# Attention scored and normalised for two groups of queries at a time, over 88 columns for each 32 queries instead of 118 for each 64, with the value products two visits behind the scores

## The chip, the cores and the metric

The kernel runs on one core of a Trainium2 chip. The metric is the device time of one execution in microseconds (us). It is given as the median of three runs. The profile comes from one further execution, recorded by the hardware profiler; its span runs from the first to the last instruction. Engines are called as the profile calls them: PE (matrix products), PEld (its weight loads), DVE, ACT, POOL, and SP, which only issues transfers (DMAs).

## The reference

Inputs are q, k, v of 4 batches, 8 heads, 768 positions and 64 dimensions, and two weight matrices, 512x2048 and 2048x512. All are float32.

```
k_sum = max of k over blocks of 32 positions         # 24 per head
v_sum = mean of v over the same blocks               # 24 per head
scores_l = scale * q @ k.T      where |i - j| < 16, else -1e9
scores_s = scale * q @ k_sum.T + log(32)
a = softmax([scores_l, scores_s])
attn = a @ [v, v_sum]                                # 3072 tokens x 512
out = relu(attn @ w_in)**2 @ w_out
```

So a query sees 31 keys around it and 24 block maxima.

## The kernel before

**Groups, units, visits.** A group is 64 queries of one batch, all 8 heads; there are 48 groups, 12 in each batch. Eight groups make a unit of 512 tokens, and there are six units. The feed-forward layer goes over one unit at a time. Units 0 and 1 run plainly: for each of 16 slices f of the hidden width, FI (12 matmuls, `h`), then on ACT and DVE `r`, `gh` and `gl` (the high and the low part of the squared relu), then FO (12 matmuls into `o`). Units 2 to 5 run as two pairs through a scheme of seven products (FI `h` in L1203, FP `o` in L1317). The attention of later groups runs between them. One *visit* on PE computes the scores S of one pair of groups (L597) and the value products V of the pair before (L803). Between S and V of one pair stands the softmax:

- M (DVE, L676): scale, add the mask, copy from the score tile `att` into `p`
- X (DVE, L692): the maximum of a row
- E (ACT, L728): the exponential, one instruction for each row block, with its sum read out
- R (DVE, L740, L741): the inverse of the sum; N (DVE, L747): its product with `p`
- T (DVE, L776): transposes of 32x32 squares from `p` into `a`
- TW and TR (SP, L787, L793): store the squares of `a` to DRAM as `turn`, and fetch them back in the order in which V needs them

A group has 4 row blocks of 128 rows (two heads of 64 queries), each with 118 columns: 24 block maxima and the 94 keys that 64 queries can see. A pair therefore has 8 row blocks in two tiles `p`, two M pieces for each group, and two each of X, N and T. The columns of the second group of a pair come from a copy `kw` of its keys (KW, ACT, L621 and L622), and the maxima are moved along in `kb` by POOL (KC, L610), so that 118 columns stand side by side for each group. Groups 0 to 7 go first, alone, with the mask added by PE; groups 8 and 9 are scored alone too, into the `o` tiles.

**What sets the order.** All work is entered as tasks in a planner (`Plan`), with a cost, a key (due time from `wanted(g)`), tasks it comes after, and buffers that it takes or uses. The planner then writes one fixed order for every engine. Each engine works its list strictly in this order, waiting at semaphores; SP is one such list for all transfers. The keys and values of a batch (`batch_k`, `batch_v`) are loaded once per batch: KL loads `kb` after the last scores of the batch before, KM (DVE, L430) makes the maxima; VM on PE (L498) makes the 24 means of v.

The weights come as 64-bit words. DVE and ACT turn each slice into a high and a low part during unit 0 (L916 to L933: WM, WR, WJ, WH, WW), beside the first 14 groups' softmax.

## Time and profile before

| | |
|---|---|
| runs | 600.46, 600.50, 600.58 us; median 600.5 us |
| profiled execution, span | 599.2 us (the runs hold some 1.3 us more around the span) |
| PE busy | 584.1 us, 97% of the span |
| DVE busy | 379.7 us, 63% |
| ACT busy | 354.8 us, 59% |
| mean granted PE clock | 0.997 of full speed |

The profiled execution has no time beside its span. A busy share is the time in which at least one instruction of the engine is under way. The granted clock is what the chip let PE have in a stretch, 1.00 for 2.4 GHz and 0.5 for 1.2 GHz. In the views, "idle before <-X" says what ended the idle time.

### The profile page before, as it was taken

Reading aid. Unit: us, or ns where it says so; the run is one execution under the profiler, and the core shown is the slowest. Engines: PE = TensorE matmul, PEld = TensorE weight load, DVE = VectorE, ACT = ScalarE, POOL = GpSimd, SP = SyncE. Lnnn points to the kernel's source line nnn. Section 1 sums busy time; section 2 is a strip of 40 time slices with the busy share of each in tenths; the row PEclk is TensorE's granted clock in tenths of the full one; section 3 lists DMA queues with packets and bytes.
Section 4 is the critical chain, followed back from the end, with each engine's and each line's share of the span. In section 5 each row is a group of like instructions: output and inputs, shape, how many; then the busy total and the mean of one; then the engine's idle time right before and its main releaser. Section 6 shows DMA issues by size and latency. Waiting matters only on the chain.

```text
span 599.2 us, 11513 instructions
## 1 busy us (share of the span) xinstructions
PE 584.1 (97%) x4132; PEld 477.3 (80%) x4132; DVE 379.7 (63%) x670; ACT 354.8 (59%) x866; POOL 66.1 (11%) x117
## 2 busy tenths in 40 slices
PE   8989999989999999999999999999999999999997
PEld 6778888858888888888878787788888888888885
DVE  5999997757547814225755958977541552349753
ACT  2999886657646635467735556656564743455542
POOL 4300004233455200000000000000000000000000
PEclk9999999989999999999999999999999999999999
DMA  8999956859987884735857956889833762126672
GB/s 307 332 392 316 371 205 211 274 162 364 343 292 249 277 282 151 264 106 151 282 157 211 291 177 205 269 257 291 276 98 105 217 209 102 35 84 203 194 231 98
DMA packets 94428, 135.43 MB, mean 226 GB/s; under 512 B 9676, under 2 KB 50636, under 8 KB 94372
## 3 DMA queue, kind: packets, MB, share of 16 engines
q1 hardware_dynamic: 94372, 134.70, 68.6%
q8 instruction: 33, 0.54, 0.4%
q14 instruction: 23, 0.19, 0.1%
HBM read 98.22 MB, written 35.65 MB: 223 GB/s over the span
## 4 chain that ended last, share of the span: by engine, by line
PE 83%; DVE 7%; ACT 5%; DMA 3%; SPq 1%; issue 1%; POOL 0%; DVEq 0%; POOLq 0%; ACTq 0%
PE h L1203 28%; PE o L1317 24%; PE o L1003 11%; PE h L979 11%; PE x L803 3%; PE att L597 2%; DMA raw<-wW 2%; PE warm L397 1%; ACT p L728 1%; DVE nm L692 1%; DMA a<-turn 1%; DVE w L933 1%; PE vps L498 1%; DVE t L925 1%; ACT w L930 1%
## 5 line engine op out<-in xcount | busy, mean ns | idle before, releaser
L1203 PE MATMUL h<-xh,w 128*128 128x512 f32 x448 | 138.8, 391 | 0.5 <-ACT r L1213 0.5
L1317 PE MATMUL o<-gh,w 128*128 128x512 f32 x448 | 120.9, 391 | 0.4 <-ACT gh L1301 0.4
L1306 DVE TENSOR_TENSOR gl<-g,gh 128x512 fp32r<-128x512 f32 x112 | 75.9, 686 | 38.3 <-ACT gh L1301 38.2
L1203 PEld LDWEIGHTS h<-xh,w 128*128 128x128 f32 x448 | 83.5, 188 | 18.7 <-ACT r L1213 1.3
L1317 PEld LDWEIGHTS o<-gh,w 128*128 128x128 f32 x448 | 83.5, 188 | 18.4 <-ACT gh L1301 0.9
L1301 ACT CAST gh<-g 128x512 fp32r<-128x512 f32 x112 | 68.8, 620 | 48.2 <-DVE gl L1306 24.9
L1203 PE MATMUL h<-xl,w 128*128 128x512 f32 x224 | 87.2, 389 | 0.0
L1213 ACT ACTIVATE r<-h 128x512 f32<-128x512 f32 x64 | 38.0, 596 | 77.9 <-PE h L1203 64.6
L979 PE MATMUL h<-xh,w 128*128 128x512 f32 x240 | 74.3, 391 | 0.0
L728 ACT ACTIVATE p<-p,nm 128x118 f32<-128x118 f32 x160 | 61.1, 387 | 17.1 <-DVE nm L692 17.0
L1317 PE MATMUL o<-gl,w 128*128 128x512 f32 x224 | 69.5, 391 | 1.0 <-DVE gl L1306 0.9
L1003 PE MATMUL o<-w,gh 128*128 128x512 f32 x240 | 62.7, 398 | 2.5 <-ACT gh L990 2.5
L1003 PEld LDWEIGHTS o<-w,gh 128*128 128x128 f32 x240 | 45.1, 190 | 12.4 <-ACT gh L990 2.9
L676 DVE SCALAR_TENSOR_TENSOR p<-att,mask 128x236 f32<-128x236 f32 x76 | 26.5, 395 | 44.1 <-PE att L597 43.9
L979 PEld LDWEIGHTS h<-xh,w 128*128 128x128 f32 x240 | 44.8, 188 | 9.6 <-DVE xl L870 0.3
L1317 PEld LDWEIGHTS o<-gl,w 128*128 128x128 f32 x224 | 41.8, 188 | 10.7 <-DVE gl L1306 2.2
L1203 PEld LDWEIGHTS h<-xl,w 128*128 128x128 f32 x224 | 42.0, 188 | 8.8
L979 PE MATMUL h<-xl,w 128*128 128x512 f32 x120 | 46.7, 389 | 0.0
L993 DVE TENSOR_TENSOR gl<-r,gh 128x512 fp32r<-128x512 f32 x30 | 22.4, 749 | 34.0 <-ACT gh L990 30.2
L610 POOL COPY kb<-kb 128x96 f32<-128x96 f32 x25 | 8.5, 339 | 293.0 <-ACT kw L622 121.4
L988 ACT ACTIVATE r<-h 128x512 f32<-128x512 f32 x30 | 17.9, 596 | 32.9 <-PE h L979 32.9
L1003 PE MATMUL o<-w,gl 128*128 128x512 f32 x120 | 34.0, 393 | 0.3 <-DVE gl L993 0.3
(148 smaller groups left out, 842.0 us busy)
## 6 DMA issues: line engine op xcount, KB each, us to landing
raw<-wW SPq DMA_DIRECT2D x32, 512.0 KB, 7.3
w<-scr_s SPq DMA_DIRECT2D x64, 256.0 KB, 2.8
w<-scr_a SPq DMA_DIRECT2D x48, 256.0 KB, 3.6
turn<-a SPq DMA_DIRECT2D x160, 64.0 KB, 2.2
a<-turn SPq DMA_DIRECT2D x40, 256.0 KB, 4.1
w<-scr_i SPq DMA_DIRECT2D x40, 256.0 KB, 3.0
v<-vS SPq DMA_DIRECT2D x33, 192.0 KB, 3.8
kb<-kT SPq DMA_DIRECT2D x16, 384.0 KB
```

Source lines behind the costliest of these rows:

```text
L676: nc.vector.scalar_tensor_tensor(out=pr.tile[:, j, :KEYS], in0=x, scalar=SCALE, in1=mask_of(g)[0].unsqueeze(1).broadcast_to([P, x.shape[1] ...
L728: nc.scalar.activation(x, score_tile(g, p % parts)[:, p] if by_pe else x, AF.Exp, bias=nm.tile[:, p : p + 1], scale=SCALE if by_pe else 1. ...
L803: nc.tensor.matmul(x_of(i)[h % 2 * D : (h % 2 + 1) * D, h // 2, :], lhsT=v_bufs[g].tile[:KEYS, h * D : (h + 1) * D], rhs=av[:KEYS, 2 * c : ...
L979: nc.tensor.matmul(cut(h), lhsT=lhs.tile[:, k * P : (k + 1) * P], rhs=rhs[:, k, c0 : c0 + n], start=(i == 0), stop=(i == 3 * KT - 1),)
L988: t2 = add(f"RL{name}", "ACT", act, lambda: nc.scalar.activation(cut(r), cut(h), AF.Relu), due + 3, [t1], take=[r], use=[h])
L993: lambda: nc.vector.tensor_tensor(out=cut(gl), in0=cut(r), in1=cut(gh).bitcast(F32), op=ALU.subtract),
L1003: nc.tensor.matmul(o_of(o, t), lhsT=terms[i][0].tile[:, (t - t0) * P : (t - t0 + 1) * P], rhs=terms[i][1].tile, start=(first and i == 0), ...
L1203: nc.tensor.matmul(h.tile, lhsT=lhs.tile[:, k * P : (k + 1) * P], rhs=rhs[:, k, c0 : c0 + TU], start=(i == 0), stop=(i == 3 * KT - 1),)
L1213: t2 = add(f"RL{name}", "ACT", 0.56, lambda: nc.scalar.activation(r.tile, h.tile, AF.Relu), due + 3, [t1], take=[r], use=[h])
L1301: f"GH{s}_{n}", "ACT", 0.54, lambda x=x, gh=gh: nc.scalar.copy(out=gh.tile, in_=x.tile), due - 4, ready,
L1306: lambda x=x, gh=gh, gl=gl: nc.vector.tensor_tensor(out=gl.tile, in0=x.tile, in1=gh.tile.bitcast(F32), op=ALU.subtract),
L1317: nc.tensor.matmul(o.tile[:, d], lhsT=chunk.tile[:, w * HALF + d * P : w * HALF + (d + 1) * P], rhs=y.tile, start=begins and w == 0 and y ...
```

## The change

- From group 8 on, the two groups of a pair share one softmax. The score tile has 8 blocks of 128 rows, and each row block holds four times 32 queries. Each 32 queries see 88 columns: 24 maxima and 64 keys. A matmul scores 32 queries of one head against 128 columns, given as two runs of 64 keys in `ends` (`kb` with 40 columns in front): the first run ends in the 24 maxima and begins with 40 columns that nobody reads.
- One M, X, N and T for the pair and eight E; `p` is a single tile, transposed at 96 columns. `turn` takes 3 of 4 blocks of squares per store, 4 stores for the pair, two fetches; the blocks that stay zero are cleared once at the start (4 transfers).
- KW is gone, KC is gone for groups after 6. One half mask of 88 columns replaces the third mask; windows at the edge of a batch are masked by two DVE memsets.
- From pair (14, 15) on (`DEEP`), values come two visits behind the scores: S of (14, 15) stands alone, each later visit has S of pair n and V of pair n-2, and two V stand alone at the end. Keys move by `AHEAD`, and the sums of v (`SUMS_AT`) stand at other visits.

```diff
+AHEAD = 21.0
+DEEP = 14
+SUMS_AT = 0, 0, 2, -2
...
+            if g % 2:
+                p_bufs[g] = buf("p", 1, (P, H, 3 * SQ), F32, f"p{g}", fixed=True)
+                a_bufs[g] = buf("a", 2, (P, 2 * DM), F32, f"a{g}", fixed=True)
...
+    def pair_keys(rows, p, k0):
+
+        x = ends[rows, p * (NB + S) : p * (NB + S) + HALF_W]
+        return bass.AP(x.tensor, x.offset, [x.ap[0], [FRONT + NB + k0, 2], [1, HALF_W]])
+
+    def pair_scores(both):
+
+        for i, g in enumerate(both):
+            k0 = TQ * (g % NW) - WINDOW + 1
+            for h in [(p, p + 1) for p in range(0, NPAIR, 2)]:
+                for half in range(2):
+                    for p in h:
+                        for r in range(2):
+                            a, m, c = square_of(2 * p + r, i)
+                            rows = slice(r * D, (r + 1) * D)
+                            first = c * TQ + half * SQ
+                            nc.tensor.matmul(
+                                s_bufs[g][0].tile[first : first + SQ, a, m * P : (m + 1) * P],
+                                lhsT=q_bufs[g].tile[rows, p, half * SQ : (half + 1) * SQ],
+                                rhs=pair_keys(rows, p, k0 + half * SQ), start=True, stop=True,
+                            )
...
+        def masked():
+            nc.vector.scalar_tensor_tensor(
+                out=pr.tile[:, :, PAD:], in0=pair_tile(g)[:, :, FRONT:], scalar=SCALE,
+                in1=half_mask.unsqueeze(1).broadcast_to([P, H, COLS]), op0=ALU.mult, op1=ALU.add,
+            )
...
+        t_e = [add(f"E{g}_{n}", "ACT", 0.36, lambda n=n: exps(n), due - 12 + 0.1 * n, [t_x], use=[pr, nm]) for n in range(H)]
...
+        def store():
+            for i in range(NSQ):
+                to = d.tile[::2, :, i, :] if i % 2 else d.tile[:3, :, i, :]
...
-            deps += keys_of(then[0], range(NPAIR)) + [t_QL[then[1]], window(then[1])] + [t_T[g] for g in both]
+            deps += keys_of(then[0], range(NPAIR)) + [t_QL[then[1]]]
...
+                if g == DEEP:
+                    scores_first([g, g + 1])
+                else:
+                    i = g - (2 if g < DEEP else 4)
+                    visit([i, i + 1], [g, g + 1], sums)
+                pair_softmax([g, g + 1])
                 done_g += 2
                 if done_g == NG:
+                    visit([g - 2, g - 1])
                     visit([g, g + 1])
```

Three places show what the planner makes of it. The first is PE late in unit 0, where pair (14, 15) is scored. `att` is the score tile, `x` what V writes, `gh_12` the high part of slice 12. Before:

```order
L1003 MATMUL o_67<-w_1253,gl_11_1491 128x512 x2
L1003 MATMUL o_66<-w_1253,gl_11_1491 128x512 x2
L597 MATMUL att_68<-kb,q_1057 64x118
L597 MATMUL att_69<-kb,q_1057 64x118
...
L803 MATMUL x_1540<-a_1409,v_83 64x64 x8
L803 MATMUL x_1540<-a_1433,v_84 64x64 x8
```

Now:

```order
L1131 MATMUL o_66<-w_1194,gl_9_1346 128x512 x2
L1131 MATMUL o_67<-w_1194,gl_9_1346 128x512 x2
L676 MATMUL att<-kb,q_1364 32x128 x16
L676 MATMUL att<-kb,q_1373 32x128 x16
L1107 MATMUL h_10_1444<-xh,w_1037 128x512 x2
```

These scores moved from behind FO of slice 11 to behind FO of slice 9 and stand without a V. 32 matmuls of 32 queries and 128 columns replace 16 of 64 and 118.

The second place is ACT, where the same pair's exponentials (E) stand among the feed-forward layer's work (`r`, `gh`). Before:

```order
L930 CAST w_1536<-t_1513 128x2x512
L1088 CAST cr_1484<-cs_1485 128x1024
L867 CAST xh<-x_1540 128x4x128
L621 COPY kw_1596<-kb 128x4x24
L622 COPY kw_1596<-kb 128x4x94
L728 ACTIVATE p_85,nm_81<-p_85,nm_81 128x118 x4
L728 ACTIVATE p_86,nm_79<-p_86,nm_79 128x118 x4
L988 ACTIVATE r_13_1634<-h_13_1576 128x512
```

Now, the next pair's exponentials (16, 17) at the place where r of slice 13 is made:

```order
L1118 CAST gh_12_1576<-r_12_1542 128x512
L1116 ACTIVATE r_13_1579<-h_13_1526 128x512
L1216 CAST cr_1514<-cs_1515 128x1024
L1117 ACTIVATE r_13_1579<-r_13_1579 128x512
L1118 CAST gh_13_1635<-r_13_1579 128x512
L995 CAST xh<-x_1584 128x4x128
L856 ACTIVATE p_80,nm_83<-p_80,nm_83 128x88 x5
```

Before, r and gh of slice 13 are queued behind eight exponentials; now they stand ahead of them, and the two KW copies are gone.

The third place is SP, with the stores of one pair's squares (`turn`) and the last weights (`raw`). Before:

```order
L913 DMA raw_1406<-wW 128x512
L913 DMA raw_1406<-wW 128x512
L787 DMA turn_1427<-a_1409 32x4x128 x4
L787 DMA turn_1435<-a_1433 32x4x128 x4
L913 DMA raw_1456<-wW 128x512
```

Now:

```order
L1041 DMA raw_1438<-wW 128x512
L593 DMA q_1457<-qW 128x256
L593 DMA q_1460<-qW 128x256
L1041 DMA raw_1463<-wW 128x512
L887 DMA turn_85<-a_81 32x3x256 x4
L1041 DMA raw_1463<-wW 128x512
```

Four stores stand between the last weights where there were eight.

## Rows read from the trace of the kernel before

**Rows 1.** The page: busy time and share, PE to POOL.
```profile
PE 584.1 (97%) x4132; PEld 477.3 (80%) x4132; DVE 379.7 (63%) x670; ACT 354.8 (59%) x866; POOL 66.1 (11%) x117
```
**Rows 2.** Windows of 20 us: busy us (instructions) by engine, clock, DMA share, GB/s.
```profile
20.00:40.00 20.00, 16.83 (x301) 14.21 (x302) 19.66 (x52) 19.75 (x71) 3.29 (x9) 1.00 0.96 353
...
60.00:80.00 20.00, 20.00 (x89) 16.54 (x90) 19.92 (x32) 17.30 (x38) 0.00 (x0) 1.00 0.96 330
...
120.00:140.00 20.00, 17.25 (x123) 13.20 (x122) 13.05 (x22) 10.59 (x30) 8.44 (x10) 0.91 0.66 215
...
300.00:320.00 20.00, 19.53 (x141) 15.98 (x140) 12.49 (x25) 9.24 (x28) 0.00 (x0) 1.00 0.63 190
320.00:340.00 20.00, 19.51 (x141) 15.68 (x140) 12.42 (x22) 11.12 (x30) 0.00 (x0) 1.00 0.75 224
...
360.00:380.00 20.00, 18.63 (x177) 14.59 (x175) 18.61 (x36) 13.10 (x37) 0.78 (x2) 1.00 0.70 220
380.00:400.00 20.00, 19.90 (x142) 15.97 (x141) 17.26 (x34) 12.57 (x33) 0.27 (x1) 1.00 0.81 249
```
**Rows 3.** The same view of two windows of 2 us.
```profile
124.00:126.00 2.00, 2.00 (x7) 1.47 (x5) 1.97 (x2) 1.97 (x3) 1.56 (x2) 0.55 0.35 96
126.00:128.00 2.00, 1.71 (x6) 1.01 (x5) 2.00 (x4) 0.09 (x1) 0.00 (x0) 0.60 0.25 66
```
**Rows 4.** Chain that ended last, 105 to 127 us: start, us, what.
```profile
104.62 5.53 DMA raw<-wW
...
115.47 1.14 DVE cs L1091
116.61 0.62 DVE p L676 x2
117.23 0.60 DVE xl L870
117.83 0.56 DVE nm L692
...
118.42 3.12 ACT p L728 x16
...
126.10 0.66 DVE gl L993
```
**Rows 5.** Who waited for whom: PE's longest wait.
```profile
PE o L1003 <- ACT gh L990: 2.5, 1, 2.5
```
**Rows 6.** Chain that ended last: a visit, the sums of v, a lone V.
```profile
57.90 0.97 PE att L597 x32
58.87 1.08 PE x L803 x32
59.95 2.94 PE h L979 x12
62.90 2.72 PE o L1003 x12
...
227.24 1.44 PE vps L498 x48
```
**Rows 7.** PE matmuls of line 597 under way (x), in windows of 0.03 us.
```profile
57.80:57.83 0.03, 0.00 (x0) 1.00 0.72 273
57.83:57.86 0.03, 0.03 (x4) 1.00 1.23 478
```
**Rows 8.** Groups of instructions: busy us, mean ns of one, idle before.
```profile
L676 DVE SCALAR_TENSOR_TENSOR p<-att,mask 128x236 f32<-128x236 f32 x76 | 26.5, 395 | 44.1 <-PE att L597 43.9
L692 DVE TENSOR_REDUCE nm<-p 128x4 f32<-128x472 f32 x40 | 25.3, 635 | 0.3
L728 ACT ACTIVATE p<-p,nm 128x118 f32<-128x118 f32 x160 | 61.1, 387 | 17.1 <-DVE nm L692 17.0
L747 DVE TENSOR_TENSOR p<-p,nm 128x472 f32<-128x472 f32 x40 | 28.5, 713 | 1.0
L776 DVE STREAM_TRANSPOSE a<-p 128x512 f32<-128x512 f32 x40 | 28.3, 708 | 1.1 <-issue 0.4
L622 ACT COPY kw<-kb 128x376 f32<-128x376 f32 x19 | 9.7, 510 | 0.0
```
**Rows 9.** PE in time, 37 to 39 us: start, us, what [idle before <-releaser].
```profile
37.83 0.50 PE L979 MATMUL h_0b<-xh,w 128*128 128x256 f32 x2 [0.80 <-ACT xh L867]
```

More of the change, by code (lines that the diff above doesn't have):

```diff
@@ L34 @@
 FIRST_S = 10
-PE_MASKS = 8
 SINGLE = 3
@@ L266, in h_buf @@
         return buf("h", 2, (P, cols), F32, name, ps)
-    att = [ps.tile([P, 2, 256], F32, name=f"att{i}", bufs=1) for i in range(2)]
+    att = ps.tile([P, 2, DM], F32, name="att", bufs=1)
     def s_buf(name):
@@ L396, in mm @@
         def mm():
[L397 to L399 removed]
+            nc.tensor.matmul(x.tile, lhsT=ident(), rhs=ident(), start=True, stop=True)
+        add(f"Y{i}", "PE", 0.42 if i < COLD else 0.22, mm, 1000 + i, [t_ident], take=[x], use=[first])
     for i in range(WARM):
@@ L597, in scores @@
                         nc.tensor.matmul(
-                            score_at(g, part, j)[c * TQ : (c + 1) * TQ, :],
-                            lhsT=q_bufs[g].tile[rows, p, :] if term else unscale[rows, :],
-                            rhs=(
-                                mask_of(g)[0][rows, :] if not term
-                                else windows[g].tile[rows, p, :] if g in windows else kb[rows, p, k0 : k0 + KEYS]
-                            ),
-                            start=term, stop=not (by_pe and term),
-                        )
+                            score_tile(g, part)[c * TQ : (c + 1) * TQ, j, :],
@@ L607, in move @@
     def move(g):
[L609 removed]
+        k0, nxt = (first_key(w, S) for w in (g % NW, g % NW + 1))
         nc.gpsimd.tensor_copy(out=kb[:, :, nxt : nxt + NB], in_=kb[:, :, k0 : k0 + NB])
[L612 to L624 removed]
@@ L692, in most @@
                 nc.vector.tensor_reduce(
-                    out=m, in_=score_tile(g, i)[:, js] if by_pe else pr.tile[:, js, :KEYS], op=ALU.max, axis=AX.X, negate=True
+                    out=m, in_=score_tile(g, i)[:, js], op=ALU.max, axis=AX.X, negate=True
                 )
-                if by_pe and not one:
+                if not one:
                     nc.vector.tensor_scalar_mul(m, m, SCALE)
             t_x.append(add(
-                f"X{name}", "DVE", 0.07 + 0.48 / parts + 0.2 * (by_pe and not one), most, due - 13, [t_m[-1]],
-                take=[] if i else [nm], use=[x] + [nm] * bool(i),
+                f"X{name}", "DVE", 0.07 + 0.48 / parts + 0.2 * (not one), most, due - 13, [t_s],
+                take=[] if i else [nm], use=[s] + [nm] * bool(i),
             ))
@@ new lines, in softmax, with turn, turned @@
+        at_ps = h_buf(f"t{g}")
+        def turn():
+            for p in range(NPAIR):
+                nc.tensor.transpose(
+                    out=at_ps.tile[:, p * P : (p + 1) * P], in_=pr.tile[:, p, :], identity=ident()
+                )
+        t_T[g] = add(f"T{g}", "PE", 0.5, turn, due - 9, [t_n, t_ident], take=[at_ps], use=[pr, first])
+        def turned():
+            nc.scalar.copy(
+                out=a.tile.rearrange("k (i n r) -> k n i r", i=NSQ, n=NPAIR),
+                in_=at_ps.tile.rearrange("k (n i r) -> k n i r", n=NPAIR, i=NSQ),
+            )
@@ L843, in products @@
                     mm()
-            for g in then:
-                scores(g, range(NPAIR), False)
+            if then:
+                pair_scores(then)
             values(both, x_of)
@@ L853, in visit @@
             block_sums_done(t_v)
-        for f in means_too:
-            f()
+        waiting.extend(means_too)
+        if then and then[-1] // NW in t_VS:
+            for f in waiting:
+                f()
+            waiting.clear()
         for g in then:
```

334 lines of the change are left out of this document (200 added, 134 removed).

## Prediction

> **What bounds the kernel now.** I read the page's busy line first. PE is busy 584.1 of 599.2 us [rows 1]; DVE and ACT have a third of the span free. Only what PE does, waits for, or does at half clock can move the time.
>
> The table of windows comes next. Between 20 and 40 us PE is busy 16.83 us, so it idles 3.17, while DVE and ACT are busy 19.66 and 19.75 of 20. From 40 us on, PE idles in five windows only: 2.75 (120 to 140), 0.47 and 0.49 (300 to 340), 1.37 and 0.10 (360 to 400), together 5.18 us [rows 2]. Between 60 and 80 us DVE is busy 19.92 and PE does not wait: a full DVE alone is no loss.
>
> The stall at 120 to 140 is the largest. The waits name PE's `o` of L1003, held 2.5 us by ACT's `gh` [rows 5]. Behind it the granted clock is 0.55 and 0.60 for two windows of 2 us [rows 3], mostly the lower level, 1.2 GHz; PE had idled before it fell. The clock thus cost (1 - 0.55) x 2.00 + (1 - 0.60) x 1.71 = 1.6 us more, and the place 2.75 + 1.6 = 4.3 us in all.
>
> The chain of waits says how the stall comes about [rows 4]. A weight transfer takes 5.53 us. DVE works on it (`cs`, up to 116.6), and only then comes to M, `xl` and X of the pair just scored. The eight exponentials run on ACT from 118.42 for 3.12 us, and `r` and `gh` of slice 13 are queued behind them; `gl` ends at 126.8. The stall belongs to a softmax wedged into the feed-forward layer's chain on ACT.
>
> **The change part by part.**
>
> *Scores on PE.* Now a scoring is 32 matmul records (16 matmuls) in 0.97 us. The sums of v are 48 records of 128 columns in 1.44 us [rows 6]. Both run four tiles at once: in one window of 0.03 us four records of L597 start, none being under way in the window before [rows 7]. So 8 rounds of 118 columns take 0.97 and 12 of 128 take 1.44. With a fixed part a and b for a round of 128 columns: a + 8 x (118/128) x b = 0.97 and a + 12b = 1.44, which gives b = 0.10 and a = 0.22. The new scoring is 64 records of 128 columns in tiles half as wide. If eight run at once, it is 8 rounds again: 0.22 + 8 x 0.102 = 1.03, or 0.06 more. There are 19 scorings of pairs: +1.1. V keeps its matmuls (1.08 [rows 6]). One burst more stands in the order, because a lone S and two lone V replace one lone V. Leaving a burst costs the FI behind it 2.94 - 2.72 = 0.22 us [rows 6]: +0.2, bounds 0 and 0.44, since entering may cost as much. The term is +1.4 in all.
>
> No row shows eight tiles. The lower bound for a scoring is no addition. The upper bound is a record's mean now, 0.97/32 = 30 ns, with 64 of them: 1.94 us, +0.97 each, +18.4 in all. I take +0.06, since four starts inside 0.03 us [rows 7] show that the tiles do not queue behind one issue of 30 ns. The Trainium skill ("TensorE: Matmul & The Clock Gate", section "Wait — 56ns, not 53.3ns?") says otherwise: starts never come closer than about 25 ns, however few the columns. The window with four starts in 0.03 us [rows 7] contradicts it for separate tiles; no row here tests it for eight.
>
> *DVE.* Per pair now: 4 M of 0.395, 2 X of 0.635, 2 N of 0.713, 2 T of 0.708 [rows 8], 5.69 us. Columns per row fall from 8 x 118 = 944 to 8 x 88 = 704 (M, X, N) and from 1024 to 768 (T): by the column 4.26 us, 1.4 less, and half as many instructions can only lower it. Over 20 pairs that frees 28 us or more on DVE. On the time it counts at nothing by itself: PE's own work covers it, as it covers the full DVE at 60 to 80 us [rows 2].
>
> *ACT.* The 160 exponentials stay but shrink from 118 to 88 columns: between 0.387 (all fixed) and 0.387 x 88/118 = 0.289 us each [rows 8], so 0 to 16 us less; I take 4, near the upper price, because a small instruction's time is mostly fixed. The KW copies go: 19 x 0.510 = 9.7 us for the larger of the two [rows 8]. This too is hidden, except where ACT is waited for, which is the stall.
>
> *The stall.* In the new order `r` and `gh` of slice 13 stand ahead of the next pair's exponentials on ACT, the KW copies that stood there are gone, and four stores on SP instead of eight stand between the last weights. With values two visits behind, the V of a visit no longer needs the softmax that has just begun. The steps from `cs` to `gl` [rows 4] then leave PE's path: -4.3 us, since without the idle PE keeps its clock. The bounds are -4.3 and 0 (the wait stands elsewhere, the second rival).
>
> *The other waits of PE.* They are 5.18 - 2.75 = 2.4 us [rows 2]. Those from 300 to 400 us lie where a visit meets late inputs; one visit more (and a shorter DVE chain) should take most: -1.5, bounds -2.4 and 0.
>
> *New waits.* The lone S of (14, 15) is put behind FO of slice 9, and its exponentials fall near `gh` of slices 10 and 11. They are at worst 8 x 0.387 = 3.1 us [rows 8] in front of an FO. While they run, PE has an FI of 2.94 [rows 6] to cover all but 0.2. The keys of the next batch also have to land sooner, since S runs ahead of V by a visit while it still follows the batch's last S. I allow +1.0 for both, bounds 0 and the old stall's 4.3.
>
> *Startup.* `h_0b` waits 0.80 us for `xh` on ACT [rows 9], and 3.17 idle lies in that window. Groups 8 and 9 are now one pair: fewer DVE instructions and no KW. Against it, four transfers that clear `turn` stand on SP ahead of the first weights, and the shared M, X, N and T give their first result later than the first of two halves did. I take -0.5, bounds -2.5 (the larger part of the 3.17) and +1.
>
> *Sum.* 599.2 + 1.4 - 4.3 - 1.5 + 1.0 - 0.5 = 595.3 us of span. The profiled execution has no time of its own beside its span; the runs' median is 1.3 us above it. That makes 596.5 us for the runs. With the small terms at half their bounds, this case's own range is 594 to 599.
>
> **The rivals.**
>
> *First, the tiles: slower.* Records in eight narrow tiles start no faster than now on average, 30 ns. A scoring then takes 1.94 us, and 18.4 replaces 1.1: 595.3 + 17.3 + 1.3 = 613.9 us. It decides from the point where a scoring costs (600.5 - 596.5)/19 = 0.21 us above my 1.03, that is from 1.24. For it: 0.97/32 and 1.44/48 are both 30 ns per record [rows 6], whatever the columns. Against it: four starts in one 0.03 us window [rows 7], and the slightly longer round that 128 columns need explains both numbers as well. By the Trainium skill's 25 ns (the same page and section) a scoring would cost 64 x 25 = 1.6 us, 0.57 above 1.03, and the run an estimated 607 us.
>
> *Second, the wait comes back.* Two visits of delay and earlier keys fill SP and ACT at other moments, and one stall of the old size (2.75 idle and 1.6 of clock) stands at another place, most likely between slices 10 and 14 or where the batch's keys change. The time is 596.5 + 4.3 = 600.8 us; with none of the other waits gone 602.3, and with two places 605. For it: DVE and ACT are still full up to about 120 us, and one late `gh` costs its idle and then the clock [rows 3, 5]. Against it: 1.4 us or more of each pair leave DVE just there, and 0.5 us of KW leave ACT.
>
> *Third, more goes.* All waits after 40 us vanish (-5.18 and the clock's 1.6), no new one comes, and startup gives its 2.5: 599.2 + 1.4 - 6.8 - 2.5 + 1.3 = 592.6 us. For it: DVE and ACT bound the startup [rows 2], and both get less work. Against it: the weight transfers, which the change leaves as they are, stand at the head of the chain [rows 4].
>
> **How the numbers follow.** The forecast has 56%, the tiles 9%, the returning wait 26%, and the larger gain 9%. A measurement of this kernel can tell about 0.2%, or 1.2 us, from no change. Faster (under 599.3) are the larger gain, nearly all of the forecast and a fifth of the second rival: 0.70. Within 0.2% is about half of the second rival: 0.13. Slower are the rest of it and the tiles: 0.17. The range of 593.0 to 602.0 leaves out the tiles, the second rival's upper third and half of the third's.
>
> **What would show it.** In the profile after, a scoring in the chain should take 1.0 to 1.1 us; 1.24 or more means the first rival. PE's busy time should be 584.1 + 1.4 - 1.6 = 583.9 us. Between 120 and 140 us PE should be busy over 19.5 of 20 at a clock of 1.00, and no wait of `o` on `gh` should exceed 1 us. If one of some 2.5 us stands at another slice with a clock below 0.7 behind it, the second rival holds. M, X, N and T of a pair should sum to at most 4.3 us. Between 20 and 40 us PE's idle should be 2 to 4 us; under 1 speaks for the third rival. The forecast is wrong in its core if the stall is gone and the time is still above 599.

## The result, and the profile after

On one chip, side by side, the changed kernel takes 605.21 us (median of 20 runs) and the kernel before 601.22 us (20 runs). The ratio is 1.0061, with a 95% interval of 1.0042 to 1.0079: slower by 0.6%. The forecast was 596.5 us, with a range of 593.0 to 602.0; the measured time lies outside the range, and the sign was wrong. The profiled execution took 605.35 us with a span of 603.6 us, so it stands for the median; its span is 4.4 us above the 599.2 of before. One execution, the profiled one of best_guess, took 1172.79 us; it is left out of all numbers below.

The page of the kernel after, with busy time and share, to be read against [rows 1]:

```profile
PE 585.8 (97%) x4772; PEld 479.8 (80%) x4772; DVE 343.3 (57%) x526; ACT 340.6 (56%) x828; POOL 61.4 (10%) x101
```

DVE lost 36 us of work and ACT 14, and yet the kernel became slower. Next come windows of 20 us in the columns of [rows 2], then four of 2 us and one of 80 in the same view:

```profile
20.00:40.00 20.00, 14.25 (x310) 12.09 (x311) 14.61 (x40) 16.07 (x57) 2.46 (x4) 0.93 0.83 290
40.00:60.00 20.00, 20.00 (x99) 17.55 (x98) 18.36 (x30) 18.45 (x44) 0.00 (x0) 0.90 0.88 322
...
100.00:120.00 20.00, 17.02 (x175) 13.30 (x177) 13.93 (x21) 15.23 (x49) 2.88 (x4) 1.00 0.73 242
120.00:140.00 20.00, 18.10 (x227) 14.23 (x208) 11.79 (x15) 8.86 (x27) 8.91 (x8) 1.00 0.81 262
300.00:320.00 20.00, 20.00 (x217) 16.47 (x216) 12.72 (x21) 12.39 (x38) 0.00 (x0) 1.00 0.87 297
360.00:380.00 20.00, 20.00 (x176) 16.35 (x175) 18.04 (x29) 13.26 (x36) 0.00 (x0) 1.00 0.79 230
...
36.00:38.00 2.00, 1.02 (x19) 0.59 (x17) 2.00 (x6) 1.75 (x4) 0.00 (x0) 0.75 1.03 418
38.00:40.00 2.00, 1.56 (x18) 1.45 (x19) 0.64 (x2) 1.22 (x3) 0.00 (x0) 0.50 1.02 412
40.00:42.00 2.00, 2.00 (x11) 2.00 (x10) 2.00 (x6) 1.71 (x4) 0.00 (x0) 0.50 1.02 413
42.00:44.00 2.00, 2.00 (x11) 2.00 (x11) 2.00 (x4) 1.54 (x3) 0.00 (x0) 0.54 1.07 405
...
20.00:100.00 80.00, 74.25 (x796) 62.45 (x797) 71.29 (x116) 64.64 (x155) 5.97 (x6) 0.96 0.84 288
```

Read PE's busy time and the clock together. From 20 to 40 us PE idles 20.00 - 14.25 = 5.75 us. Then the granted clock is 0.50, the level of 1.2 GHz, for most of 37 to 44 us, behind the idle. That costs 1.02 x 0.25 + 1.56 x 0.50 + 2.00 x 0.50 + 2.00 x 0.46 = 2.96 us more. The table has both numbers, worked out in this way in windows of 2 us, for each stretch: the idle of PE, and what the lower level of the clock costs.

| stretch | before: idle, clock | after: idle, clock | difference |
|---|---|---|---|
| 0 to 20 us | 2.32, 0 | 2.73, 0 | +0.4 |
| 20 to 60 us | 3.17, 0 | 5.75, 2.96 | +5.5 |
| 100 to 150 us | 2.76, 1.58 | 5.00, 0 | +0.7 |
| 300 to 420 us | 2.44, 0 | 0, 0 | -2.4 |
| the rest of the span | 586.9 | 587.2 | +0.2 |

So three things happened. The startup got 5.9 us longer. The stall late in unit 0 did not go. The later waits all went. PE's waits after:

```profile
PE h L1107 <- ACT r L1116: 3.8, 2, 3.0
PE t L803 <- DVE qvpa_lent L792: 2.7, 1, 2.7
...
PE att L676 <- DVE nm L863: 1.0, 1, 1.0
```

The wait of `o` on `gh`, 2.5 us [rows 5], is gone. A wait of `h` on `r` of 3.0 us stands at 111 to 114 us, some 10 us earlier (PE went on at 123.39 us before, and at 113.69 now); the 1.90 us that PE idles from 120 to 140 are mostly the 1.0 of `att` on `nm` and the rest of the 3.8. The wait of 2.7 on `qvpa_lent` is new and lies at 33 to 36 us.

The costs of the new operations came out close to their terms. The chain of one visit, as in [rows 6]:

```profile
65.03 1.09 PE att L676 x64
66.12 1.08 PE x L912 x32
67.20 2.99 PE h L1107 x12
```

A scoring takes 1.09 us (1.03 forecast). Eight tiles do run at once, as the matmul records of L676 under way in one window of 0.03 us show, to be read against the four of [rows 7]:

```profile
65.03:65.06 0.03, 0.03 (x8) 0.03 (x16) 1.00 1.62 546
```

64 starts in 1.09 us are 17 ns each. So the first rival, which needed 30 ns, fails. The estimate from the 25 ns of the Trainium skill ("TensorE: Matmul & The Clock Gate", section "Wait — 56ns, not 53.3ns?") fails here too, by the same 17 ns. DVE and ACT, by groups of instructions, to be read against [rows 8]:

```profile
L831 DVE SCALAR_TENSOR_TENSOR p<-att,half_mask 128x704 f32<-128x704 f32 x19 | 16.9, 888 | 41.0 <-PE att L676 40.7
L850 DVE TENSOR_REDUCE nm<-p 128x8 f32<-128x704 f32 x20 | 17.6, 878 | 0.1
L856 ACT ACTIVATE p<-p,nm 128x88 f32<-128x88 f32 x160 | 57.0, 358 | 20.1 <-DVE nm L850 20.1
L869 DVE TENSOR_TENSOR p<-p,nm 128x704 f32<-128x704 f32 x20 | 17.8, 892 | 0.5
L876 DVE STREAM_TRANSPOSE a<-p 128x768 f32<-128x768 f32 x20 | 19.5, 974 | 0.3
```

A pair now takes 0.888 + 0.878 + 0.892 + 0.974 = 3.63 us of DVE where it took 5.69. An exponential shrank by 29 ns, 4.6 us in all, near the 4 us taken.

**Where the startup went.** SP, in order of time (start, us spent issuing, what). Before:

```profile
21.01 0.43 SPq L913 DMA_DIRECT2D raw<-wW  x1
21.76 1.68 SPq L552 DMA_DIRECT2D qvpa_lent<-fv_lent  x2
23.49 0.51 SPq L913 DMA_DIRECT2D raw<-wW  x1
```

After:

```profile
20.98 3.43 SPq L467 DMA_DIRECT2D turn<-a  x4
24.46 1.62 SPq L611 DMA_DIRECT2D qvpa_lent<-fv_lent  x2
26.13 2.23 SPq L1041 DMA_DIRECT2D raw<-wW  x2
```

The four transfers that clear `turn` hold SP for 3.43 us. The second weight transfer, which was issued at 21.01 us before, is issued at 26.13, 5.1 us later. DVE then waits for weights, and PE for DVE (kernel after, in time; idle before and its releaser in brackets):

```profile
30.32 0.43 DVE L1047 TENSOR_SCALAR raw<-raw 128x512 uint32<-128x512 uint32 x1 [1.43 <-DMA raw<-wW]
...
33.43 0.43 DVE L1047 TENSOR_SCALAR raw<-raw 128x512 uint32<-128x512 uint32 x1 [2.08 <-DMA raw<-wW]
...
35.66 0.63 PE L803 MATMUL t<-first,qvpa_lent 128*128 128x128 f32 x4 [2.68 <-DVE qvpa_lent L792]
```

What PE waits for is N of one of the first groups, the product in its `p` (`qvpa_lent` is memory lent to these groups). In DVE's list it stands behind the second of these two waits, and behind the 0.89 us of M of the new pair (8, 9). That is how a late transfer becomes an idle PE.

**Where the late stall went.** DVE, ACT and PE around 110 us, kernel after, in time:

```profile
105.42 0.17 DVE L862 TENSOR_SCALAR nm<-nm 128x8 f32<-128x8 f32 x1 [3.00 <-ACT p L856]
...
109.71 0.37 ACT L856 ACTIVATE p<-p,nm 128x88 f32<-128x88 f32 x1 [3.15 <-DVE nm L850]
...
112.54 0.60 ACT L1118 CAST gh<-r 128x512 fp32r<-128x512 f32 x1
113.05 0.59 ACT L1116 ACTIVATE r<-h 128x512 f32<-128x512 f32 x1
...
113.69 0.73 PE L1107 MATMUL h<-xh,w 128*128 128x512 f32 x2 [2.98 <-ACT r L1116]
```

ACT idles 3.15 us until DVE has the maxima of pair (14, 15). Then eight exponentials run, and only behind them `gh` and `r`, for which PE waits. This is the old stall at another pair: a softmax wedged into the feed-forward layer's chain on ACT, late because DVE was late.

Why DVE was late there, the first of these lines says in part. The next row in DVE's list is R of the pair before, (12, 13), and DVE stands idle for 3.00 us while ACT runs all eight exponentials of that pair. Only then come its R, N and T, and behind them M and X of (14, 15). Before, with a softmax in two halves, DVE worked on the second half meanwhile; at the old stall it waited 0.38 us:

```profile
120.07 0.61 DVE L740 TENSOR_SCALAR nm<-nm 128x4 f32<-128x4 f32 x1 [0.38 <-ACT p L728]
```

Between 100 and 130 us DVE waits 4.2 us for exponentials in after, and 0.4 in before. No run split the shared softmax again, so what this alone costs is not shown.

### The profile page after: what moved, and what is told of

The parts are those of the page before. It is cut to its first block, busy times and chain, and to the rows that moved or that the text cites. A ratio compares the mean times of both kernels' runs of the same rounds, so it can differ in the third digit from the quotient of the medians.

```text
span 603.6 us, 12465 instructions
## 1 busy us (share of the span) xinstructions
PE 585.8 (97%) x4772; PEld 479.8 (80%) x4772; DVE 343.3 (57%) x526; ACT 340.6 (56%) x828; POOL 61.4 (10%) x101
## 4 chain that ended last, share of the span: by engine, by line
PE 85%; issue 5%; DMA 4%; DVE 2%; POOL 1%; SPq 1%; ACT 1%; POOLq 0%; DVEq 0%; ACTq 0%
PE h L1332 29%; PE o L1446 25%; PE o L1131 12%; PE h L1107 11%; PE x L912 3%; PE att L676 3%; DMA qvpa_lent<-vF 2%; DMA raw<-wW 1%; DMA fv_lent<-vS 1%; POOL cs L1213 1%; PE vps L552 1%; PE h_1a L1107 0%; POOL cr L1198 0%; DVE t L1053 0%; PE h_0b L1107 0%
## 5 line engine op out<-in xcount | busy, mean ns | idle before, releaser
L856 ACT ACTIVATE p<-p,nm 128x88 f32<-128x88 f32 x160 | 57.0, 358 | 20.1 <-DVE nm L850 20.1
L1121 DVE TENSOR_TENSOR gl<-r,gh 128x512 fp32r<-128x512 f32 x30 | 23.8, 797 | 29.6 <-ACT gh L1118 27.0
L831 DVE SCALAR_TENSOR_TENSOR p<-att,half_mask 128x704 f32<-128x704 f32 x19 | 16.9, 888 | 41.0 <-PE att L676 40.7
L1198 POOL TENSOR_TENSOR cr<-w 128x512 f32<-128x512 f32 x16 | 24.7, 1565 | 108.0 <-DVE w L1061 93.6
```

The costliest lines, as they stand in the source:

```text
L856: nc.scalar.activation(x, x, AF.Exp, bias=nm.tile[:, n : n + 1], accum_out=nm.tile[:, H + n : H + n + 1])
L1121: lambda: nc.vector.tensor_tensor(out=cut(gl), in0=cut(r), in1=cut(gh).bitcast(F32), op=ALU.subtract),
L1198: nc.gpsimd.tensor_tensor(out=raw.tile[:, k * DM : (k + 1) * DM], in0=ws[k][0].tile.bitcast(F32), in1=ws[k][1].tile.bitcast(F32), op=ALU.add)
```

## The experiments

Four theories of the loss stood against each other: the clearing transfers on SP (*clears*), the exponentials of pair (14, 15) ahead of `gh` and `r` (*exps*), the two visits of delay (*lag*), and, from the second set of runs on, a page of PE's own instructions that comes late (*code*). Ratios are to the kernel before, run beside each set, with 95% intervals. "Idle" and "clock" are worked out as in the table above, from the profile of one execution each.

### First set: the clears and the exponentials

**clear_later** issues the clears on SP behind the weights of slice 7.

```diff
+MOVES = [(["turns"], "WL1_7")]
...
-        for t in plan.order():
+        for t in moved(plan.order(), MOVES):
```

> The changed kernel with one move: the four transfers that clear turn stand on SP behind the weights of slice 7, not ahead of the second weight transfer; every other row of every engine as in the changed kernel. Theory (the four transfers, 3.4 us on SP at 20.9 us, make the weights of slices 0 and 1 late, and this costs 3.0 us of PE idle and 3.0 of half clock before 60 us): PE idle from 20 to 40 us falls from 5.75 to about 3.2, the clock stays at 1.00 to 60 us, and the time falls by 5 to 8 us, the upper part of that if DVE and ACT, started sooner, also shorten the wait of FI at 110 us. Rival (the shared softmax of groups 8 and 9 gives its result later and holds up the startup by itself): idle stays above 5 us and the time within 1.5 us of the changed kernel's.

**before_clears** adds four like transfers, to a buffer that nobody reads, to the kernel before, at the place where after has them.

```diff
+    def clear_same():
+        x = blank.rearrange("c (i e) -> c i e", i=2)
+        for j, i in ((1, 1), (4, 0), (1, 1), (4, 0)):
+            nc.sync.dma_start(out=same[j, :, i::2, :], in_=x)
+MOVES = [(["same"], "QL9")]
```

> The kernel before with four transfers of the same size and form added on SP at the same place, behind the q of group 9 and ahead of the second weight transfer (they write 64 KB each to memory that nobody reads); nothing else moved. Theory (the transfers alone make the startup late): slower than before by 3 to 7 us, with PE idle from 20 to 40 us at 5 or more and some half clock there. Rival (it is the shared softmax): within 1.5 us of before.

**exp_behind** puts the exponentials of pair (14, 15) behind `gh` of slice 10 and `r` of slice 11 on ACT (and R and N with them).

```diff
+MOVES = [([f"E15_{n}" for n in range(8)], "RL0_11"), (["R15"], "E15_7"), (["N15"], "R15")]
```

> The changed kernel with one move: on ACT the eight exponentials of pair (14, 15) stand behind gh of slice 10 and the first relu of slice 11, not ahead of them. Theory (ACT sat 3.15 us waiting for that pair's maxima and then 2.8 us in its exponentials while FI of slice 12 waited for the relu): the wait of 3.0 us of FI on ACT's r at 110 us falls below 0.7 us and the time falls by 2 to 3 us. Rival (the exponentials only come later, and their values or the next scoring wait in their place): the wait moves to another line and the time stays within 1 us.

**both_moves** has both lists of moves.

> Both moves at once: the clearing transfers behind the weights of slice 7, and the exponentials of (14, 15) behind gh of slice 10 and relu of slice 11. If the two costs are independent: their gains add up, 7 to 10 us faster than the changed kernel, about 596. If the second stall is a child of the first (DVE and ACT late from the startup on): within 1 us of the first move alone.

| run | us (runs) | ratio | 20 to 60 us: idle, clock | 100 to 150 us: idle, clock |
|---|---|---|---|---|
| clear_later | 604.94 (12) | 1.0046 [1.0024, 1.0068] | 6.29, 0 | 4.61, 1.67 |
| before_clears | 605.99 (12) | 1.0069 [1.0042, 1.0097] | 6.27, 2.21 | 3.05, 1.56 |
| exp_behind | 603.98 (12) | 1.0033 [1.0005, 1.0060] | 3.31, 1.54 | 5.02, 0 |
| both_moves | 603.09 (12) | 1.0030 [1.0006, 1.0054] | 5.27, 0 | 5.25, 0 |

before_clears shows that four such transfers at this place are enough: the kernel before becomes as slow as after, by 4.1 us, with 8.5 us lost between 20 and 60 us as after loses 8.7. It is not the same case in small, though. Its SP and PE, in time:

```profile
20.62 5.93 SPq L440 DMA_DIRECT2D same<-xl  x4
26.60 0.58 SPq L564 DMA_DIRECT2D q<-qW  x1
27.23 1.17 SPq L939 DMA_DIRECT2D raw<-wW  x1
28.44 1.62 SPq L578 DMA_DIRECT2D qvpa_lent<-fv_lent  x2
...
32.52 1.12 PE L829 MATMUL att<-qvpa_lent 118*64 118x64 f32 x16 [3.79 <-issue]
```

The four transfers hold SP for 5.93 us here, not 3.43, and PE's long stop is another one. It stands in front of the value products of groups 4 and 5, and the view names no releaser. These products read what the two small transfers `qvpa_lent<-fv_lent` bring, which here stand behind the four; by the trace the first was complete at 32.43 us, and PE goes on at 32.52. So PE waited for these, and not for weights by way of DVE as in after.

To move them away in after gains almost nothing (clear_later; 5 to 8 us were expected), and that is the surprise. The weights were on time, yet PE, in time, did this:

```profile
27.34 1.16 PE L691 MATMUL o<-kb,q 64*32 64x128 f32 x64
31.72 1.15 PE L927 MATMUL att<-qvpa_lent 118*64 118x64 f32 x32 [3.22 <-DVE p L846]
```

The view names DVE's `p` as the releaser, but that work was long done. exp_behind's profiled execution (601.08 us, 2.9 under its median) has SP's clears at 2.58 us instead of 3.43, and only 4.9 us lost at the start where after lost 8.7; so the size of the startup loss varies by some 4 us between executions with the order of SP unchanged. less_dve below, with this order too, lost 4.8. The execution profiled of after lay at its median (605.35 and 605.21), but its 8.7 us are one execution's. In the late stretch the wait of `h` on `r` is gone, and two others hold PE as long. PE's waits in exp_behind:

```profile
PE att L691 <- DVE p L884: 2.6, 1, 2.6
PE x L927 <- DMA a<-turn: 2.2, 1, 2.2
```

The *exps* theory named the wait rightly and its worth wrongly: idle at 100 to 150 us is 5.02 where it was 5.00. both_moves is 1.9 us under clear_later, neither the 7 to 10 us under after of two independent costs nor the same as clear_later.

### Second set: a plain startup, the rest of SP, the lag

**start_as_before** has the clears late and also the second weight transfer ahead of the small transfers, as before has it. It tells the weights from the *code* theory.

```diff
+MOVES = [(["turns"], "WL1_7"), (["WL0_1"], "QL9")]
```

> The changed kernel with two moves on SP alone: the four clearing transfers behind the weights of slice 7, and the second weight transfer ahead of the two small ones (fv_lent, 24 rows), so that the first weights stand as in the kernel before. Theory (the weights' and the small transfers' place on SP, with PE's own code loads queued among full transfers, make the startup): PE idle from 20 to 60 us falls from 5.8 to 3 to 4 us with the clock at 1.00, and the time is 601 to 603. Rival (PE's code: twice as many records in a scoring bring the third 16 KB page sooner than the full queues can load it, wherever the weights stand): idle stays at 5 to 6 us, 604 to 605.

**late_sp** has both_moves and another order on SP from 100 to 125 us: the q of groups 18 and 19 directly behind the stores of pair (14, 15), the weights of slice 14 behind the fetch of pair (12, 13), and the plain copies of the weights later.

```diff
+MOVES = [..., (["QL18", "QL19"], "V13"), (["WA1"], "WS0"), (["WL0_14", "WL1_14"], "TR13")]
```

> Both earlier moves (clearing later; exponentials of (14, 15) behind gh of 10 and relu of 11), and on SP between 100 and 125 us: the q of groups 18 and 19 directly behind the stores of pair (14, 15), the last two weight transfers (slice 14) behind the fetch of pair (12, 13), and the plain copies of the weights (scr_a) later. Theory (with the exponentials moved, PE waits 2.2 us for a fetched turn and 2.5 for q only because SP holds them behind weights and scratch stores): both waits fall below 1 us, idle from 100 to 150 us from 5.2 to under 2, and the time is 3 to 4 us under both moves' 603.1: about 599.5. Rival (DVE and ACT are simply late there and any wait removed comes back under another name): idle stays at 4 or more, time within 1 us of 603.1.

**all_moves** has late_sp and start_as_before together.

> All moves together: start as before, clearing later, exponentials behind, and the SP order from 100 to 125 us. If startup and late stall are independent and both theories hold: 596 to 598, faster than both kernels. If the late stall only moves: 600 to 602.

**deep20** begins the two visits of delay at pair (20, 21); the planner writes its own order.

```diff
-DEEP = 14
+DEEP = 20
```

> The changed kernel with values one visit behind up to group 19 and two from group 20 on (one number changed, everything planned anew), so no scoring stands alone in unit 0; clearing transfers where the change has them. If the early second visit of delay is what costs at 100 to 130 us (the lone scoring and its exponentials ahead of gh of 10): idle there falls from 5.0 to 3 or less, the time by 2 us or more. If it is the transfers and the engines being late, idle stays at 4 to 6 us and the time within 1.5 us of 605.2.

| run | us (runs) | ratio | 20 to 60 us: idle, clock | 100 to 150 us: idle, clock |
|---|---|---|---|---|
| start_as_before | 606.49 (6) | 1.0108 [1.0078, 1.0139] | 5.72, 0 | 5.03, 0 |
| late_sp | 608.02 (6) | 1.0121 [1.0093, 1.0149] | 6.03, 1.62 | 7.61, 2.94 |
| all_moves | 608.52 (6) | 1.0124 [1.0103, 1.0146] | 5.19, 1.65 | 6.94, 1.68 |
| deep20 | 605.52 (6) | 1.0079 [1.0055, 1.0103] | 3.54, 1.65 | 3.37, 1.66 |

The delay is not the cause of the loss: deep20 is as slow as after, though its late idle of 3.37 us lies between the two that were expected. The wait behind the first scoring stays 3.4 us in start_as_before, so the weights' place isn't its cause either. late_sp missed: it left a load of `v` behind the fetch, and one wait of PE took all back:

```profile
PE x L927 <- DMA v<-vS: 4.4, 1, 4.4
```

What was left for the wait was PE's own instructions. The transfers view has a queue called "instruction". In clear_later, 26 to 29 us and then 29 to 30.1 us (packets, MB, share of 16 engines in each):

```profile
q1 hardware_dynamic: 372, 1.09, 99.3%
...
q8 instruction: 1, 0.02, 5.3%
```

No packet of the queue moves from 26 to 29 us, while the weights fill the engines to 99%. Then one of 16 KB lands, at 30.04, and PE's next matmul starts at 31.72. The packet ended 1.4 to 1.7 us ahead of PE's next matmul in each trace where the two were compared: 30.70 and 32.12 in before, 28.01 and 29.59 in after, 30.68 and 32.24 in start_as_before, 29.87 and 31.43 in late_sp2 below. PE's stop comes at nearly the same place in its list each time, behind 932 records of matmuls and weight loads in before and 936 in the others. Before has it too, as its PE in time shows, 0.62 us without any releaser:

```profile
32.12 0.39 PE L979 MATMUL h_0a<-xh,w 128*128 128x256 f32 x1 [0.62 <-issue]
```

The queue's packets fit PE's list: the page of the profile counts 33 in before and 38 in after, for 2 x 4132 and 2 x 4772 records of PE and PEld, some 250 to a packet. So PE's instructions seem to come in pages, and the wait to be for one of them; the third set tries this. At this place the new kernel scores groups 8 and 9 together, with 64 matmul records and 64 weight loads. The old one scored group 8 alone, with 16 and 16. PE therefore comes to that page's end at about 28.5 us instead of 31.5, while the page's packet stands behind the weights. The Trainium skill ("Runtime: NRT & Kernel Launch", section "Instruction fetch mechanics") describes such pages, of 16 KiB and 256 instructions, which an engine fetches ahead through its own queue, and calls the crossing mostly hidden. The size agrees with the packets here; hidden it is not, with 0.6 us in before and 3.2 in clear_later.

### Third set: the page's end moved

**code_early** is clear_later with the first 16 of the warm-up matmuls, whose results nobody reads, cut into three small ones each. That adds instructions before the startup and moves every page's end some 128 records forward.

```diff
-            nc.tensor.matmul(x.tile, lhsT=ident(), rhs=ident(), start=True, stop=True)
+            for _ in range(3 if i < 16 else 1):
+                m, n = (32, 48) if i < 16 else (P, P)
+                nc.tensor.matmul(x.tile[:m, :n], lhsT=ident()[:, :m], rhs=ident()[:, :n], start=True, stop=True)
```

> clear_later (the changed kernel with the clearing transfers behind the weights of slice 7) with the first 16 warm-up matmuls each cut into three of 32 rows of output and 48 columns, which adds 32 matmuls, 128 of PE's instructions, and so moves the ends of its 16 KB pages of code 128 instructions forward; every order is otherwise that of clear_later. Theory (the wait of 3.4 us of the value products of groups 4 and 5 near 28 us, put down to a DVE instruction, is PE's next page of code, asked for at 24 us and loaded behind full weight transfers at 29.1 us, always some 1.45 us before PE goes on): the wait falls below 0.8 us, idle from 20 to 60 us falls from 6.3 to 3 to 4, and the time by 2 to 3.5 us to about 602. Rival (it is the small transfers or DVE): the wait stays at 2.5 us or more and the time within 1 us of 604.9.

**late_sp2** is late_sp with the loads of `v` of groups 15 and 16 moved forward too, and one of the two weight transfers of slice 14 left where it was.

```diff
+MOVES = [..., (["QL18", "QL19", "LV15"], "V13"), (["LV16"], "TR15"), (["WA1"], "WS0"), (["WL1_14"], "TR13")]
```

> Both moves (clearing later, exponentials behind) and another SP order from 105 to 125 us: the q of groups 18 and 19 and the v of 15 directly after the stores of pair (14, 15), then the fetch of that pair, the v of 16, the combined weights, and the plain copies last; the second weight transfer of slice 14 behind the fetch of pair (12, 13). Theory (late_sp lost its gain to the v of group 15, which I had left behind the fetch, and to both weights of slice 14; q alone would gain): no wait of a scoring on q or of a V on v above 0.7 us, idle from 100 to 150 us falls from 5.2 to 3 or less, and the time from 603.1 to about 600.5. Rival (DVE and ACT are late there and every wait removed comes back under another name): idle 4.5 or more, time 602 or more.

**best_guess** has late_sp2 and code_early together.

> late_sp2 and the code moved forward, together. If both theories hold: 597.5 to 599, faster than both kernels (601 and 605). If only the code's: about 600.5. If neither: 603.

| run | us (runs) | ratio | 20 to 60 us: idle, clock | 100 to 150 us: idle, clock |
|---|---|---|---|---|
| code_early | 606.63 (6) | 1.0085 [1.0054, 1.0115] | 4.22, 1.57 | 5.05, 4.56 |
| late_sp2 | 606.83 (6) | 1.0084 [1.0054, 1.0115] | 4.86, 1.70 | 4.35, 3.15 |
| best_guess | 608.58 (5) | 1.0112 [1.0081, 1.0143] | - | - |

Nothing is read from a trace of best_guess. All three missed the times that were expected. PE of code_early, in time:

```profile
27.66 1.16 PE L693 MATMUL o<-kb,q 64*32 64x128 f32 x64
28.75 1.15 PE L929 MATMUL att<-qvpa_lent 118*64 118x64 f32 x32
```

V now runs right behind the scoring, with every order as in clear_later and only PE's pages moved: the wait was the page. Yet the kernel did not get faster. At the start PE won 2.1 us of idle, and 1.57 went to the half clock behind the idle that is left. Late it lost 3.3 us more than clear_later (5.05 + 4.56 against 4.61 + 1.67): 2.9 us of it is half clock, and a wait of `h` on `r` at 140 us grew from 0.76 to 2.30. PE's waits, with 2.75 us at 111 and 2.30 at 140:

```profile
PE h L1124 <- ACT r L1133: 5.0, 2, 2.8
```

exp_behind, late_sp and code_early each took away a wait that was named, and PE lost as much or more elsewhere in unit 0. That pointed at something behind all of these waits. A list that ACT, SP and PE all wait for in unit 0 is DVE's, with the weights and the softmax on it.

### Fourth set: DVE's work

**less_dve** is after, **before_less_dve** is before, with the join of the two words of a weight (WJ, one DVE instruction a slice) cut to 8 columns for slices 3 to 15. That leaves the low bits of those weights out, and takes 13 x (1221 - 161) ns = 13.8 us from DVE.

```diff
-            x = temp().bitcast(U32)
+            x, n = temp().bitcast(U32), k * DM if f < SINGLE else 8
...
+                out=x[:, :n], in0=x[:, :n], scalar=3, in1=words(0)[:, :n], op0=ALU.logical_shift_left, op1=ALU.bitwise_or
```

> The changed kernel with the join of the weights' words (DVE, 128x1024, 1.22 us) cut to 8 columns for slices 3 to 15; so nearly all of the joining of these weights is left out, 13 x 1.1 = 14 us of DVE between 42 and 130 us. Every order and every transfer is as in the changed kernel. Theory (DVE's lateness sets the end of unit 0): the idle and half clock from 100 to 150 us (5.0 us) fall below 1.5 and the time falls by 3 to 5 us, while the startup before 40 us stays. Rival (SP's order and the lone scoring set it): idle there stays at 3.5 us or more and the time within 1.5 us of 605.2.

> The kernel before with the same cut: the join of the weights' words on 8 columns for slices 3 to 15, 14 us of DVE less, every order the same. Theory (DVE sets the end of unit 0 here too): the stall of 2.5 us at 121 us and the half clock behind it (4.3 us together) go, and the time falls by 3.5 to 4.5 us to about 597. Rival (the softmax's own place among the feed-forward work, as the prediction had it): the stall stays at 1.5 us or more.

| run | us (runs) | ratio | 20 to 60 us: idle, clock | 100 to 150 us: idle, clock |
|---|---|---|---|---|
| less_dve | 599.89 (12) | 0.9970 [0.9947, 0.9993] | 3.23, 1.60 | 2.12, 0 |
| before_less_dve | 598.23 (7) | 0.9942 [0.9921, 0.9963] | 3.30, 0 | 1.25, 0 |

Windows of less_dve:

```profile
100.00:120.00 20.00, 19.86 (x174) 15.90 (x173) 13.78 (x20) 15.53 (x43) 0.00 (x0) 1.00 0.96 312
120.00:140.00 20.00, 18.03 (x164) 14.19 (x163) 10.11 (x16) 11.19 (x35) 12.22 (x12) 1.00 0.78 253
```

and of before_less_dve:

```profile
120.00:140.00 20.00, 18.75 (x136) 14.79 (x135) 13.47 (x22) 12.15 (x31) 8.35 (x10) 1.00 0.84 286
```

This is the only edit that shrank what is lost late, idle and clock together, and it did so in both kernels with no order changed: 5.00 to 2.12 in after, and 2.76 + 1.58 to 1.25 in before. (An idle below 1.5 was expected in after; in before, what was expected came.) By the ratios, after gains 1.0061 - 0.9970 = 0.9%, or 5.5 us; before gains 0.6%, or 3.5 us. Of the 5.5 us the profile puts 2.9 in the late stretch. Another 3.9 lie between 20 and 60 us, where the first shortened join stands at 43 us, behind the startup's idle, and single executions differ by as much.

So the late stall hangs on DVE's steps for the weights, and the named waits are places where their lateness meets PE. Whether it is the sum of DVE's work, the trial can't say. The join is also one step on the way of each slice from its landing to its low part, and that way became 1.06 us shorter 13 times. DVE is not full there either: from 100 to 120 us it is busy 13.93 of 20 in after. With the same relief the two kernels' intervals overlap, and no one stretch parts them: less_dve loses 1.5 us more at the start and 0.9 more late in unit 0, before_less_dve still waits 2.5 us from 300 to 420 us. That less_dve loses only 4.8 us at the start has to be read with its profiled execution, which lay 1.5 us under its median.

### Fifth set: the work put on POOL

**after_pool** and **before_pool** put the low step (WW) of slices 4, 6, 8, 10 and 12 on POOL, which idles then. If DVE's work is the bound, this should help.

```diff
-            nc.vector.tensor_tensor(
+            (nc.gpsimd if f in (4, 6, 8, 10, 12) else nc.vector).tensor_tensor(
```

> The changed kernel with the last step of the weights (the low part, w - its high part, 128x1024, 1.2 us on DVE) done by POOL for slices 4, 6, 8, 10 and 12 (some 3.1 us each there by the 1.57 us of POOL's 128x512); planned anew, all work done. Theory (DVE's work sets the end of unit 0; 14 us less of it gave 5.3 us): 6 us less should give about 2 us, 603 us. Rival (POOL's step is late for PE, or slows DVE beside it): 605 or more.

> The kernel before with the same five steps on POOL; planned anew, all work done. Theory (14 us less DVE work gave 3.9 us): 6 us less should give 1.5 us, about 600.3, faster than both kernels. Rival (POOL's step is late for PE, or slows DVE): 602 or more.

| run | us (runs) | ratio | 20 to 60 us: idle | 100 to 150 us: idle, clock |
|---|---|---|---|---|
| after_pool | 607.02 (10) | 1.0080 [1.0053, 1.0107] | 5.50 | 5.14, 0 |
| before_pool | 606.08 (12) | 1.0073 [1.0051, 1.0096] | 7.16 | 3.95, 1.63 |

Both missed. The step, by the groups of before_pool and its waits of PE:

```profile
L933 POOL TENSOR_TENSOR w<-t,w 128x1024 fp32r<-128x1024 f32 x5 | 17.7, 3541 | 45.1 <-ACT w L930 45.1
```

```profile
PE h L979 <- POOL w L933: 3.7, 1, 3.7
```

POOL takes 3.54 us for what takes DVE 1.2 to 1.3 (in after_pool 2.72), PE waits for it once for 3.7 us, and in after_pool DVE's join took 1615 ns instead of 1221.

These two runs bear on what the fourth set left open. after_pool hardly tests it: the longer joins gave back what was taken, and DVE is busy 91.73 us from 20 to 130 us where it was 92.21. In before_pool DVE is busy 94.09 us there instead of 99.75, so 5.7 us less, but the last step of each of the five slices is longer. Its late loss did not fall; it grew from 4.34 to 5.58 us. That speaks for the length of the way and against the sum of DVE's work. As the orders were planned anew and PE had its new wait of 3.7 us at 59 us, it does not settle it. No version tried beats both kernels with the whole computation in it.

## Why the prediction was wrong

The span came out 603.6 - 595.3 = 8.3 us above the sum. By terms: 6.4 in the startup, 4.0 in the stall and the new waits together, and 1.2 less in PE's work and 0.9 less in the other waits than was put down for them. Each of these is one profiled execution against one.

**The startup, -0.5 with a bound of +1: it was +5.9.** This is the largest miss and most of the result. The four transfers that clear `turn` were named, "on SP ahead of the first weights", but given no price of their own. They held SP for 3.43 us, the second weight transfer was issued 5.1 us later, and with the half clock behind the idle the stretch from 20 to 60 us cost 8.7 us instead of 3.2. before_clears shows that four such transfers at this place can cost as much, though it held SP longer and PE waited elsewhere. That clear_later does not bring it back is the second thing no step of the prediction had: the new scoring's records, four times as many at this place, bring PE sooner to the end of a page of its instructions, which with the weights on time lands later (3.2 us). code_early shows that this wait is the page. With both gone, 4.22 us of idle and 1.57 of clock are left against 3.17 before; what holds these is open.

**The stall, -4.3, and the new waits, +1.0: together it was +0.7.** The step "the steps from `cs` to `gl` then leave PE's path" was right by its words; that wait is gone. What failed is that the stall was taken to belong to that order. It came back some 10 us earlier at another pair, between the slices that the second rival names, and under further names when it was taken away there. The prediction saw the exponentials of (14, 15) in front of `gh` of slices 10 and 11, but priced only their own 3.1 us and let an FI cover all but 0.2. In the trace ACT stands idle 3.15 us in front of them, for DVE, and PE waits 2.98. That the shared softmax gives "their first result later" was priced for the startup alone; at this place DVE waits 3.00 us for the eight exponentials of the pair before. less_dve and before_less_dve show that DVE's steps for the weights carry most of the lateness. How it parts between these steps and the shared softmax is not shown.

**DVE's saving "counts at nothing by itself: PE's own work covers it".** The full DVE at 60 to 80 us [rows 2] costs nothing there, and it was read as a DVE that costs nothing. In unit 0 that step failed: 1.06 us less in each of 13 joins took 2.9 us off the late loss of after and 3.1 off that of before. DVE did save work, but from 20 to 100 us it stood idle for 80.00 - 71.29 = 8.7 us (the widest window shown of after) instead of 80.00 - 78.31 = 1.7 before. Of these, 3.5 us (1.43 + 2.08) are the waits for the late weights. That the saving would have reached the stall without them is not so: in start_as_before, with the weights on time, DVE still idles 80.00 - 74.06 = 5.9 us there, and the late idle is 5.03.

**The other waits, -1.5 of 2.4: right, and all 2.4 went.** The windows from 300 to 420 us show PE busy throughout. **Scores, +0.06 each: it was +0.12** (1.09 against 0.97), 19 x 0.12 = 2.3 us instead of 1.1. The rest of PE's work came out +0.2 in all, below the +1.4; what made up for the scores was not taken apart. Two of the prediction's sums are off in the last place (4.26 for 4.25, 596.5 for 596.6), which changes nothing. **The first rival** is refuted by the window with eight records. **The second** named the place, but not the form: three waits (2.98, 1.00 and 0.86 us) with the clock at 1.00, where it looked for one of some 2.5 us and a clock below 0.7 behind it. Its 600.8 us lacked the startup.

**Left open.** No run changed the page's end in the kernel before, so its 0.6 us there was not tried by itself. No run shortened the way of a weight without taking work from DVE, or split the shared softmax. less_dve still idles 2.1 us at 100 to 150 us; what sets that was not taken apart. Nor was it settled why late_sp2 and all_moves lost more late than they won, beyond the waits that their traces name; several of the late runs have only six executions, and many single ratios between them are within each other's intervals.

## What to carry to other kernels

The wait that the profile names at a stall is where lateness meets the engine that matters; shorten a step of the engine that is late, as a trial, before an order is changed to remove the wait. When two halves of a chain become one, ask what the engine between them does while it waits for the whole. Price every transfer on a queue by what stands behind it, the first loads above all: four small ones made the kernel before 4.1 us slower. Where a change multiplies the instructions of an engine, look where its pages of instructions end and what the transfer engines do then.

## What the runs showed of the hardware

- PE's instructions come in packets of 16 KB. Where one stood behind full transfer queues, PE stopped for 3.2 us in clear_later and 3.4 in start_as_before, and went on 1.4 to 1.7 us after the packet had landed. The waits view put this down to another engine.
- A clearing transfer of 64 KB held SP for 3.43/4 = 0.86 us in the profile of after (5.93/4 = 1.5 in before_clears), one of 512 KB of weights for 0.43 us in before.
- Eight tiles of 64x32 take 64 matmul records of 128 columns in 1.09 us, 17 ns from start to start on average.
- A subtraction of 128x1024 took POOL 2.7 us in after_pool and 3.5 in before_pool, and DVE 1.2 to 1.3.
